# An alignment directive ahead of attention's second product, in an attention and channel-mix kernel

## The chip, the cores and the metric

The kernel runs on one core of a Trainium2 chip. The metric is the device time of one execution in microseconds, the median of several runs; lower is better. TensorE (PE in the profile) multiplies, and its weight loads are shown apart (PEld); VectorE is DVE, ScalarE is ACT, GpSimd is POOL, and SyncE (SP) issues the transfers.

## The reference

Attention over pooled keys and values feeds an RWKV channel mix. Batch 8, 8 heads, 576 tokens, head size 64; keys and values are averaged over groups of 8, which leaves 72 keys for each head.

```python
k_p = k.reshape(B, H, Sp, pool, D).mean(axis=3)
v_p = v.reshape(B, H, Sp, pool, D).mean(axis=3)
scores = scale * np.matmul(q, k_p.transpose(0, 1, 3, 2))
attn = softmax(scores)                       # over the 72 keys
x = np.matmul(attn, v_p)                     # (B, S, 512) after heads are joined
x_prev = x shifted by one token, zero at each batch's first
xk = mu_k * x + (1.0 - mu_k) * x_prev
xr = mu_r * x + (1.0 - mu_r) * x_prev
k = np.maximum(xk @ w_k, 0.0)                # 512 -> 1024
v = k * k @ w_v                              # 1024 -> 512
r = 1.0 / (1.0 + np.exp(-(xr @ w_r)))        # 512 -> 512
out = r * v
```

## The kernel before

The 4608 tokens are worked through in 13 chunks: 128, 256, and eleven of 384 tokens (chunks 2 to 12). For a chunk, attention comes first. `scores` multiplies queries by keys (line 769, tile `quad`), a softmax follows on DVE, ACT and POOL, and `quarters(c)` multiplies the weights of attention by the values: attention's second product (line 1000). It is written as one burst of 96 small matmuls, on quarters of the PE array, one after the other with nothing between; its operands are f32. I call the burst that makes chunk c "burst c"; there are eleven, 2 to 12.

Out of the burst's result ACT, POOL and DVE make the shifted mixes xk and xr, each split in a high and a low part so that products can run in the faster f32r format with three terms (`terms`). Then PE multiplies for the mix. `hidden(c, jt)` for jt 0 to 7 is x times w_k, 12 matmuls of 384 columns each (line 1146, tile `mm`); `gate(c, tt)` is x times w_r, 36 for a chunk (line 1195); `mixed(c, tt)` is the product by w_v, 72 for a chunk (line 1228).

The order of instructions is set while the kernel is written out. Each of these functions is a generator that gives its engine and an assumed length, and `Order.run` picks by due times which goes next. On PE this comes to a fixed round for chunks 4 to 11: `hidden(c, 0)` to `hidden(c, 7)`, burst c+1, `gate(c, ...)`, the first two thirds of `mixed(c, ...)`, a block of `scores`, the rest of `mixed`, and in some chunks a second block of scores. A burst starts right behind `hidden(c, 7)` and the gate starts right behind the burst. Every engine works its own instructions in order.

`hidden(c, jt)` takes one of three PSUM banks named `mm`; its matmuls for jt 4 first wait for DVE to have emptied that bank.

Of the kernel before, what the change touches and what calls it, by code (L numbers as in the profile page):

```python
# [25 lines left out]
NCT = DM // P  # L26
NJT = DF // P
# [4 lines left out]
CHUNKS = [128, 256] + [384] * 11  # L32
# [80 lines left out]
}  # L113
PLAN = ""
SPARE = 0.5
SECOND = 0.0
NEXT = 14.0
ATT = [0.0, 10.0]
# [117 lines left out]
def dve(n, lock=True):  # L236
    return "dve", 0.067 + n / 960, lock


def act(n, func=None):  # L240
    return "act", 0.1 + n / 1200, False, func
# [6 lines left out]
def pe(n, whole=False, times=1):  # L248
    return "pe", times * (2 * max(0.111, n / 1200 + 0.003) if whole else max(0.111, n / 2400 + 0.0135)), False
# [3 lines left out]
def attention_then_channel_mix(  # L253
# [13 lines left out]
    nc = tc.nc  # L267
# [41 lines left out]
    def operand(kind, c):  # L309
        if c in WHOLE:  # L310
            return whole_operands[kind]
        if (kind, c) not in operands:
            whole = {"pth": range(len(CHUNKS)), "xkh": WHOLE_HID, "xrh": WHOLE_GATE, "sh": WHOLE_MIX, "ptq": range(len(CHUNKS))}.get(kind, ())
            dtype = F32 if c in whole else F32R
            operands[kind, c] = sb.tile(shapes[kind], dtype, name=f"{kind}_{c}", tag=kind)
        return operands[kind, c]
# [7 lines left out]
    def before(kind, c):  # L324
        return every(kind, c - 1) if c > 1 else []

    def free_of_early(c, tag):
        kept = c in {"sl": WHOLE_MIX, "xrl": WHOLE_GATE}[tag]
        return [("early", t, i) for t, n in EARLY for i in range(n) if t == tag and not kept]
# [387 lines left out]
    def softmax(i):  # L717

        parts = tiles[i][2]
        if leads(i - 1):  # L720
            yield need(("scores", i, 0))
            yield from part(i, 0, 2)
            return
        group = [i, i + 1] if leads(i) else [i]
        if i:
            yield need(("scoring", i - 1))
            c = tiles[max(group[-1] - 2, 0)][0] - 1
            if c >= 0 and c not in WHOLE_ATT:
                yield need(("attended", c, 0))
        yield need(("q", i), *[("keys", b, p) for b, *_ in parts for p in range(1 if i in HALVED else 2)])  # L730
        pair = None
        if i in BESIDE:
            pair = [(yield take("mm")), (yield take("mm"))]
            sc = None
            halves = [t.rearrange("p (a n) -> p a n", a=1) for t in pair]
        else:
            sc = yield take("sc")
            halves = [sc[:, a:a + 1] for a in range(2)]
        held["halves", i] = sc, pair, halves
        if i in HALVED:  # L740
            for kind in ("mx", "e", "sm", "px", "pm"):
                held[kind, i] = yield take(kind)
        if leads(i):
            yield need(
                ("emptied", i - 1, 0), ("q", i + 1), *[("keys", b, p) for b, *_ in tiles[i + 1][2] for p in range(2)]
            )
            hi = yield take("hi")
            held["halves", i + 1] = hi, None, [hi[:, a:a + 1] for a in range(2)]
            order.make(("scoring", i + 1))
        order.make(("scoring", i))  # L750
        if i in HALVED:
            yield from part(i, 0, 1)
        else:
            yield from part(i, 0, 2)
# [226 lines left out]
    def quarters(c):  # L981

        yield need(*ready(c))
        sc = yield take("sc")
        hi = yield take("hi")
        yield "pe", 2.75, False
        main = operand("pth", c).rearrange("p g n -> p (g n)").rearrange("p (i j k) -> p i j k", j=16, k=32)
        rest = operand("ptq", c)
        out = quad[:, :, :CH].rearrange("p t (g i k) -> p t g i k", g=NPAIR, k=32)
        batch = [next(b for b, _, n, at in units[c] if at <= CH // 4 * t < at + n) % 2 for t in range(4)]  # L990
        for g in range(NPAIR):
            for j in range(3):
                for t, i in enumerate(batch):
                    rows = slice(32 * t, 32 * t + 32)
                    for m in range(2):
                        if j < 2:
                            w, p = vq_main[i][rows, (t - 2 * m - j) % 4, g], main[rows, :, 4 * g + 2 * m + j, :]
                        else:
                            w, p = vq_rest[i][rows, g // 2, 2 * (g % 2) + m], rest[rows, :, g // 2, :]
                        nc.tensor.matmul(  # L1000
                            out=out[m * D:(m + 1) * D, t, g], lhsT=w, rhs=p, start=(j == 0), stop=(j == 2),
                        )
        for g in range(NPAIR):
            held["out", c, g] = quad[:, :, g * CH // 4:(g + 1) * CH // 4]
            order.make(("attended", c, g))
        held["quad", c] = [sc, hi, NPAIR]
# [117 lines left out]
    def hidden(c, jt):  # L1124
        n = CHUNKS[c]
        whole = c in WHOLE_HID
        if jt:
            yield need(("hiding", c, jt - 1))
        elif c > 1:
            yield need(("mixing", c - 1, CHUNKS[c - 1] // P - 1))  # L1130
        yield need(("full" if whole else "parts", "k", jt), *([("x", c, 0, 0)] if c < 2 else []))
        bank = yield take("mm")
        order.make(("hiding", c, jt))
        hp = bank[:, :n]
        for ct in range(NCT):
            yield need(("x", c, ct, 0))
            o = slice(ct * P, (ct + 1) * P)
            yield pe(n, whole, 1 if whole else 3)
            if whole:
                terms = [(full["k", jt], operand("xkh", c))]  # L1140
            else:
                h, l = high["k", jt], low["k", jt]
                xh, xl = operand("xkh", c), operand("xkl", c)
                terms = [(h, xh), (l, xh), (h, xl)]
            for k, (w, x) in enumerate(terms):
                nc.tensor.matmul(  # L1146
                    out=hp, lhsT=w[:, o], rhs=x[:, ct, :n],
                    start=(ct == 0 and k == 0), stop=(ct == NCT - 1 and k == len(terms) - 1),
                )
        order.make(("hid", c, jt))  # L1150
        yield need(*before("mixed", c), *free_of_early(c, "sl"))
        sh = operand("sh", c)[:, jt]
        kept = c in WHOLE_MIX
        rk = sh if kept else (yield take("rk"))
        yield act(n)
        nc.scalar.activation(out=rk[:, :n], in_=hp, func=AF.Relu)  # L1156
        if c < 2 and jt < SQUARED_ON_ACT[c]:
            order.give("mm", bank)
            yield act(n)
            nc.scalar.activation(out=rk[:, :n], in_=rk[:, :n], func=AF.Square)  # L1160
        else:
            yield dve(n, False)
            nc.vector.scalar_tensor_tensor(  # L1163
                out=rk[:, :n], in0=hp, scalar=0.0, in1=rk[:, :n], op0=ALU.max, op1=ALU.mult
            )
            order.give("mm", bank)
        if not kept:
            yield act(n)
            nc.scalar.copy(out=sh[:, :n], in_=rk[:, :n])  # L1169
            yield dve(n)  # L1170
            nc.vector.tensor_tensor(  # L1171
                out=operand("sl", c)[:, jt, :n], in0=rk[:, :n], in1=sh[:, :n], op=ALU.subtract
            )
            order.give("rk", rk)
        order.make(("s", c, jt))
# [76 lines left out]
    for b, i in first_tile.items():  # L1252
        c = tiles[i][0]
# [15 lines left out]
    for i in range(NT):  # L1269
        spare = SPARE if tiles[i][0] > 1 else 0.0  # L1270
        order.add(tile_due[i], softmax(i), spare)
# [6 lines left out]
    for c, n in enumerate(CHUNKS):  # L1278
        if c not in WHOLE_ATT:
            order.add(att_due[c], quarters(c), SPARE)  # L1280
        for g in range(NPAIR):
            order.add(att_due[c] + g, attended(c, g), SPARE if c > 1 else 0.0)
            if c in WHOLE:
                order.add(att_due[c] + g + 6, later_joined(c, g))
        for jt in range(NJT):
            order.add(begin[c] + 0.0455 * n * jt / NJT, hidden(c, jt), 1.0 if c else 0.0)
        for tt in range(n // P):
            order.add(begin[c] + 0.0455 * n + 2.8 * tt, gate(c, tt))
            order.add(begin[c] + (0.0455 + 0.022) * n + 5.5 * tt, mixed(c, tt))
# [56 lines left out]
```

## Time and profile before

| | us |
|---|---|
| runs | 613.98, 614.94, 616.98 |
| median | 614.94 |
| span of the profiled execution, first to last instruction | 612.4 |

Of the profiled execution the span is what is given; the median run lies 2.5 us over it, which is taken as what lies around the span. PE is busy for 592.1 us of it, DVE for 354.3, ACT for 296.1 and POOL for 221.4.

In the views, `L1000 PE MATMUL quad<-pth,vq_main` is line 1000's matmul that writes tile `quad` out of `pth` and `vq_main`. `[1.52 <-issue]` says that the engine was idle for 1.52 us before this instruction and that the profile shows nothing that it waited for. An f32 matmul runs as two loads and two products, an f32r one as one of each. Queue q8 of the DMA engines carries PE's instructions to it.

### The profile page before, as it was taken

The numbers are of one execution on the slowest core, as the hardware profiler recorded it, in microseconds if no ns is written. First come the engines' busy times: TensorE is split into PE (matmuls) and PEld (weight loads), VectorE is DVE, ScalarE is ACT, GpSimd is POOL, SyncE is SP. The second block draws the span as 40 slices with busy tenths as digits, with TensorE's granted clock in tenths as the row PEclk, the third lists the DMA queues.
The fourth block names the chain that finished last, engine by engine and source line by source line (L and its number), as shares of the span: only waits on it lengthen the run. The fifth ranks groups of instructions, "written<-read, shape, count | busy, mean of one in ns | idle before, by whom it ended". The sixth has DMA issues, their size and how long they took to land.

```text
span 612.4 us, 13988 instructions
## 1 busy us (share of the span) xinstructions
PE 592.1 (97%) x5822; PEld 508.9 (83%) x5822; DVE 354.3 (58%) x709; ACT 296.1 (48%) x574; POOL 221.4 (36%) x350
## 2 busy tenths in 40 slices
PE   9989999999999899999999999999999999999997
PEld 8868457888989888988988987988977977988985
DVE  5779975976537927727726816956516825423411
ACT  3656765845462454453644444544435436335420
POOL 2411259548151555524125525355105306105000
PEclk9999999999999999999999999999999999999999
DMA  8697332342004134212005205032002000000001
GB/s 307 218 344 296 108 119 69 131 165 89 9 18 182 44 105 164 88 44 104 2 2 181 87 27 182 19 130 70 19 2 70 18 2 35 17 2 36 18 0 51
DMA packets 23054, 54.70 MB, mean 89 GB/s; under 512 B 2896, under 2 KB 6352, under 8 KB 22992
## 3 DMA queue, kind: packets, MB, share of 16 engines
q1 hardware_dynamic: 22992, 53.82, 24.9%
q8 instruction: 45, 0.74, 0.5%
q14 instruction: 17, 0.14, 0.1%
HBM read 41.23 MB, written 9.44 MB: 83 GB/s over the span
## 4 chain that ended last, share of the span: by engine, by line
PE 73%; POOL 9%; DVE 6%; issue 5%; ACT 5%; DMA 0%; POOLq 0%; DVEq 0%; ACTq 0%
PE mm L1146 31%; PE mm L1228 16%; PE mm L1195 14%; PE quad L1000 4%; POOL xkl L1120 3%; POOL xrl L1120 3%; PE quad L769 3%; DVE xm L1094 3%; ACT t L1052 2%; ACT xkh L1118 1%; PE bank L441 1%; PE mm L578 1%; POOL stage L567 1%; ACT xrh L1118 1%; PE quad L1038 1%
## 5 line engine op out<-in xcount | busy, mean ns | idle before, releaser
L1146 PE MATMUL mm<-xkh,w_k 128*128 128x384 f32 x704 | 180.1, 336 | 0.3 <-DVE rk L1163 0.2
L1228 PE MATMUL mm<-w_v,sh 128*128 128x512 f32 x528 | 167.2, 392 | 0.0
L1146 PEld LDWEIGHTS mm<-xkh,w_k 128*128 128x128 f32 x704 | 126.7, 188 | 2.3 <-DVE rk L1163 0.5
L1094 DVE SCALAR_TENSOR_TENSOR xm<-quad,given,t 128x384 f32<-128x384 f32 x88 | 50.4, 613 | 126.4 <-ACT t L1052 89.6
L1146 PE MATMUL mm<-xkl,w_k 128*128 128x384 f32 x352 | 117.9, 335 | 0.5 <-POOL xkl L1120 0.5
L1228 PEld LDWEIGHTS mm<-w_v,sh 128*128 128x128 f32 x528 | 99.1, 188 | 21.4
L1228 PE MATMUL mm<-w_v,sl 128*128 128x512 f32 x264 | 102.9, 390 | 0.0
L1195 PE MATMUL mm<-w_r,xrh 128*128 128x512 f32 x264 | 84.3, 394 | 3.0 <-issue 1.6
L1169 ACT CAST sh<-rk 128x384 fp32r<-128x384 f32 x88 | 45.1, 513 | 64.3 <-DVE rk L1163 64.1
L1156 ACT ACTIVATE rk<-mm 128x384 f32<-128x384 f32 x88 | 43.1, 490 | 66.5 <-PE mm L1146 65.3
L1171 DVE TENSOR_TENSOR sl<-rk,sh 128x384 fp32r<-128x384 f32 x88 | 56.0, 636 | 28.4 <-ACT sh L1169 27.8
L1120 POOL TENSOR_TENSOR xkl<-xm,xkh 128x384 fp32r<-128x384 f32 x44 | 44.2, 1016 | 65.2 <-ACT xkh L1118 65.2
L1146 PEld LDWEIGHTS mm<-xkl,w_k 128*128 128x128 f32 x352 | 66.1, 188 | 1.1 <-POOL xkl L1120 1.1
L1195 PEld LDWEIGHTS mm<-w_r,xrh 128*128 128x128 f32 x264 | 49.5, 188 | 12.9 <-issue 1.7
L1163 DVE SCALAR_TENSOR_TENSOR rk<-mm,rk 128x384 f32<-128x384 f32 x88 | 48.6, 553 | 19.6 <-ACT rk L1156 19.5
L567 POOL TENSOR_TENSOR stage<-stage 128x512 f32<-128x512 f32 (+4 forms) x56 | 51.0, 913 | 20.2 <-issue 9.1
L1228 PEld LDWEIGHTS mm<-w_v,sl 128*128 128x128 f32 x264 | 49.6, 188 | 10.0
L1203 ACT ACTIVATE rs<-mm 128x512 f32<-128x512 f32 x36 | 21.5, 599 | 66.4 <-PE mm L1195 66.3
L1052 ACT ACTIVATE t<-quad,om_sb 128x384 f32<-128x384 f32 (+1 forms) x96 | 48.3, 573 | 7.7 <-PE quad L1000 4.0
L1195 PE MATMUL mm<-w_r,xrl 128*128 128x512 f32 x132 | 51.4, 390 | 0.0
L1238 DVE TENSOR_TENSOR rs<-mm,rs 128x512 f32<-128x512 f32 x36 | 24.7, 687 | 41.4 <-PE mm L1228 41.1
L856 POOL TENSOR_TENSOR px<-e,sm 128x64 f32<-128x64 f32 (+1 forms) x33 | 11.6, 352 | 102.3 <-DVE sm L850 89.4
(138 smaller groups left out, 784.4 us busy)
## 6 DMA issues: line engine op xcount, KB each, us to landing
qs<-in_qT SPq DMA_DIRECT2D x36, 256.0 KB, 3.8
out<-rs SPq DMA_DIRECT2D x36, 256.0 KB, 2.0
stage<-in_kT SPq DMA_DIRECT2D x15, 576.0 KB, 4.9
stage<-in_vm SPq DMA_DIRECT2D x15, 512.0 KB, 5.5
got_wk<-in_w_k SPq DMA_DIRECT2D x8, 512.0 KB, 7.2
got_wv<-in_w_v SPq DMA_DIRECT2D x8, 512.0 KB, 10.0
stage<-in_vr SPq DMA_DIRECT2D x6, 512.0 KB, 3.9
got_wr<-in_w_r SPq DMA_DIRECT2D x4, 512.0 KB, 7.3
```

The lines of the kernel that those rows point to most:

```text
L567: nc_eng.tensor_tensor(out=st[:, :, :w], in0=st[:, :, :w], in1=st[:, :, w:2 * w], op=ALU.add)
L1052: nc.scalar.activation(out=by_token(ts[m][:, 1:n + 1]), in_=xp, func=AF.Copy, scale=om_sb[:, m, g:g + 1])
L1094: nc.vector.scalar_tensor_tensor(out=by_token(xm[:, :n]), in0=bank[:, :n] if c in WHOLE_ATT else bank, scalar=mu_sb[:, m, g:g + 1], in1=by ...
L1120: nc.gpsimd.tensor_tensor(out=lo, in0=xm[:, :n], in1=hi, op=ALU.subtract)
L1146: nc.tensor.matmul(out=hp, lhsT=w[:, o], rhs=x[:, ct, :n], start=(ct == 0 and k == 0), stop=(ct == NCT - 1 and k == len(terms) - 1),)
L1156: nc.scalar.activation(out=rk[:, :n], in_=hp, func=AF.Relu)
L1163: nc.vector.scalar_tensor_tensor(out=rk[:, :n], in0=hp, scalar=0.0, in1=rk[:, :n], op0=ALU.max, op1=ALU.mult)
L1169: nc.scalar.copy(out=sh[:, :n], in_=rk[:, :n])
L1171: nc.vector.tensor_tensor(out=operand("sl", c)[:, jt, :n], in0=rk[:, :n], in1=sh[:, :n], op=ALU.subtract)
L1195: nc.tensor.matmul(out=bank, lhsT=x[:, ct, o], rhs=w, start=(ct == 0 and k == 0), stop=(ct == NCT - 1 and k == len(terms) - 1),)
L1228: nc.tensor.matmul(out=bank, lhsT=s[:, o], rhs=w, start=(jt == 0 and k == 0), stop=(jt == NJT - 1 and k == len(terms) - 1),)
L1238: nc.vector.tensor_tensor(out=rs, in0=bank, in1=rs, op=ALU.mult)
```

## The change

One directive on TensorE, in front of the first matmul of `hidden(c, 4)` for chunks 4 to 11, thus eight times, ahead of bursts 5 to 12. As the directive is defined, the loader of the program puts padding there, so that the instruction behind it comes to stand at a given slot of a block of 256 instructions. Up to 64 slots of padding are run as empty instructions; where more are needed, the first of them is made a branch over the rest.

The slot asked for is (45 - 96) mod 256 = 205. From there `hidden(c, 4)` to `hidden(c, 7)` issue 4 x 12 matmuls, each one load and one product: 96 instructions. The burst behind them begins at slot 45.

```diff
+BLOCK = 256
+ALIGNED_FROM = 4
+INTO_BLOCK = 45
+MOST_PADS = 64
@@ hidden(c, jt)
             yield need(("x", c, ct, 0))
             o = slice(ct * P, (ct + 1) * P)
             yield pe(n, whole, 1 if whole else 3)
+            if c >= ALIGNED_FROM and 2 * jt == NJT and ct == 0 and c + 1 < len(CHUNKS):
+                before_quarters = 3 * 2 * NCT * (NJT // 2)
+                nc.tensor.addr_align(BLOCK, (INTO_BLOCK - before_quarters) % BLOCK, MOST_PADS)
             if whole:
```

PE's order is otherwise as it was. On PE, before, where `hidden(4, 3)` ends and `hidden(4, 4)` begins (chunk 4; `mm` are the banks, `xkh` and `xkl` the parts of xk, `w_k` parts of the weights; what an instruction waits for stands behind it):

```order
L1146 MATMUL mm_118<-xkh_1872,w_k_648 128x384 x2
L1146 MATMUL mm_118<-xkl_1873,w_k_648 128x384
L1146 MATMUL mm_117<-xkh_1872,w_k_657 128x384 [waits DVE_49]
L1146 MATMUL mm_117<-xkh_1872,w_k_657 128x384
L1146 MATMUL mm_117<-xkl_1873,w_k_657 128x384
```

The same place on PE now (seven lines further down in the source); the directive is the row `ISA`:

```order
L1153 MATMUL mm_118<-xkh_1872,w_k_648 128x384 x2
L1153 MATMUL mm_118<-xkl_1873,w_k_648 128x384
L1145 ISA
L1153 MATMUL mm_117<-xkh_1872,w_k_657 128x384 [waits DVE_49]
L1153 MATMUL mm_117<-xkh_1872,w_k_657 128x384
L1153 MATMUL mm_117<-xkl_1873,w_k_657 128x384
```

The directive stands ahead of the matmul that waits for DVE. Further on, now as before, the end of `hidden(4, 7)` and the start of burst 5 on PE:

```order
L1153 MATMUL mm_117<-xkl_1873,w_k_713 128x384
L1153 MATMUL mm_117<-xkh_1872,w_k_713 128x384 x2
L1153 MATMUL mm_117<-xkl_1873,w_k_713 128x384
L1004 MATMUL quad<-pth_1817,vq_main_71 64x96 x4
L1004 MATMUL quad<-pth_1817,vq_main_72 64x96 [waits DMAHW3_49]
```

No instruction stands between the two but what the rows show, so nothing moved here but by the padding.

## Rows read from the trace of the kernel before

**Rows 1.** the page: busy time by engine, instruction queue, the last chain by engine.

```profile
PE 592.1 (97%) x5822; PEld 508.9 (83%) x5822; DVE 354.3 (58%) x709; ACT 296.1 (48%) x574; POOL 221.4 (36%) x350
...
q8 instruction: 45, 0.74, 0.5%
...
PE 73%; POOL 9%; DVE 6%; issue 5%; ACT 5%; DMA 0%; POOLq 0%; DVEq 0%; ACTq 0%
```

**Rows 2.** waits of PE, 160 to 560 us: us in total, times, longest.

```profile
PE quad L769 <- DVE xm L1094: 4.0, 7, 0.7
PE quad L1000 <- issue: 2.7, 2, 1.3
PE mm L1195 <- issue: 1.6, 1, 1.6
PE mm L1195 <- DVE ptq L923: 1.4, 1, 1.4
```

**Rows 3.** the last chain in order of time: start us, us, what; bursts 5, 7, 8, 10, 11.

```profile
208.13 2.56 PE quad L1000 x151
210.69 1.55 issue
212.25 8.48 PE mm L1195 x36
...
303.12 2.54 PE quad L1000 x145
305.65 8.42 PE mm L1195 x36
...
348.98 2.12 PE quad L1000 x124
...
353.23 8.40 PE mm L1195 x36
...
443.95 2.38 PE quad L1000 x136
...
447.90 8.36 PE mm L1195 x36
...
492.51 2.39 PE quad L1000 x137
...
496.65 8.40 PE mm L1195 x36
```

**Rows 4.** timeline of the weight loads in bursts 8 and 10.

```profile
350.68 0.23 PEld L1000 LDWEIGHTS quad<-pth,vq_main 32*64 32x64 f32 x7
352.43 0.28 PEld L1000 LDWEIGHTS quad<-pth,vq_main 32*64 32x64 f32 x19 [1.52 <-issue]
...
446.42 0.19 PEld L1195 LDWEIGHTS mm<-w_r,xrh 128*128 128x128 f32 x1
447.90 0.19 PEld L1195 LDWEIGHTS mm<-w_r,xrl 128*128 128x128 f32 x1 [1.30 <-issue]
```

**Rows 5.** L1000 alone in burst 5: stretch us, PE busy (x), PEld busy (x), clock.

```profile
208.00:212.24 4.24, 2.63 (x192) 2.44 (x192) 1.00 0.01 4
```

**Rows 6.** instruction queue in 210.0:211.1 and in 395:398.07: packets, MB, share.

```profile
q8 instruction: 1, 0.02, 5.4%
...
q8 instruction: 1, 0.02, 2.6%
```

**Rows 7.** the last chain: hidden of chunk 5, then the scores behind bursts 5 and 7.

```profile
232.31 1.23 PE quad L769 x64
...
239.24 16.67 PE mm L1146 x96
...
325.41 1.23 PE quad L769 x64
```

**Rows 8.** from burst 5 to burst 6 and burst 7 to burst 8: all engines, clock.

```profile
208.06:255.84 47.78, 45.51 (x461) 40.33 (x461) 30.27 (x54) 21.03 (x41) 28.34 (x43) 1.00 0.34 117
303.05:348.91 45.86, 45.39 (x462) 40.31 (x461) 26.47 (x51) 20.65 (x38) 19.20 (x28) 1.00 0.25 90
```

## The prediction

> **What bounds the kernel now.** I read the page first. PE is busy for 592.1 of 612.4 us, and the chain that ended last lies on PE for 73% [rows 1]. A microsecond of PE's idle time in the steady part is therefore close to a microsecond of the whole. So the next view is what PE waits for, from 160 to 560 us, which holds bursts 4 to 12. Four rows carry nearly all of it [rows 2]: scores that wait for DVE, 4.0 us in 7 times, and three rows that add up to 2.7 + 1.6 + 1.4 = 5.7 us in 4 times, at the bursts (L1000) or at the first matmul behind one (L1195). Three of those four waits are put down to "issue": nothing that the profile shows was waited for.
>
> The last chain in order of time says where they are [rows 3]. An ordinary burst takes 305.65 - 303.12 = 2.53 us until the gate starts. The other bursts look like it but for four: burst 5 takes 4.12, burst 8 353.23 - 348.98 = 4.25, burst 10 3.95 and burst 11 4.14 us. Their excess is 1.59 + 1.72 + 1.42 + 1.61 = 6.34 us.
>
> In burst 8 the pause stands in the middle of a run of loads of one kind that wait for nothing [rows 4]. In burst 10 the profile names DVE ptq [rows 2], but the load of that very product ran at 446.42, and it is the load that carries the wait. The product and the next load came at 447.90 [rows 4]. So that too is a pause between two instructions, not a wait for DVE.
>
> **What the pause is.** I counted PE's instructions in program order: a load one, a product one, a separate semaphore instruction one. A burst is 192 loads and 192 products [rows 5], 384 instructions. The whole is 11,690, and queue q8 brings them in 45 packets of 0.74 MB together [rows 1], one for every 256 or so. The first instruction behind each of the four pauses is number 4290, 7106, 9154 and 10178 in this count. Their differences are 2816, 2048 and 1024, which are 11, 8 and 4 times 256. So all four pauses stand on the same slot, where a block of 256 begins. From this the starting slots of bursts 2 to 12 follow: 86, 69, 102, **128**, 25, 51, **204**, 230, **127**, **153**, 242, the four that pause in bold.
>
> A burst issues an instruction each 2.53 / 384 = 6.6 ns, a block in 1.69 us. Burst 5 starts at 208.06 us [rows 8] in slot 128, passes a boundary after 128 instructions, at 208.9, and reaches the next at its own end, 1.69 us later. One packet comes in 210.0 to 211.1 us, with 5.4% of 16 engines for 1.1 us, thus 0.95 us long [rows 6], and PE goes on at 212.25 [rows 3]. So the block behind a boundary opened 3.3 us after the boundary before it; the same sum gives 3.2, 3.2 and 3.1 for bursts 8, 10 and 11. My reading: a block is ordered when the one before it is entered, takes 3.1 to 3.3 us, and only a burst eats a block faster than that.
>
> Bursts 9 and 12 also pass two boundaries (26 and 14 instructions in) and don't pause. For burst 9 a packet lies within 395 to 398.07 us [rows 6], before its first product at 398.07: the instructions had been taken in ahead of the array, so the order went out early. This lead matters below.
>
> The page Runtime: NRT & Kernel Launch of the Trainium skill, section Instruction fetch mechanics, says that crossing a boundary is mostly hidden, since instructions are issued more slowly than blocks arrive. By that rule there would be nothing to gain and the sum would stay at 614.9. The trace agrees for nearly all of the 45 blocks and not for these four, where the measured pauses decide.
>
> **The change, term by term.**
>
> *Bursts 5 to 12 begin at slot 45.* The 96 instructions behind the directive end there, and I found nothing else between. The boundary ahead is then 45 instructions, 22.5 matmuls of `hidden`, before the burst: 16.67 / 96 = 0.174 us each [rows 7], thus 3.9 us. The one boundary within is 211 instructions in, 1.4 us. Between them lie 5.3 us, against 3.3 needed. The next is 173 instructions of burst and 41.5 of gate's products of 8.42 / 36 = 0.234 us [rows 3] later: 1.1 + 9.7 = 10.8 us. No pause is left by this: **-6.3 us**. Bursts 6 and 7, at slots 25 and 51, ran without a pause on either side of 45. An error of a few slots in my count would not matter. Bursts 6, 7, 9 and 12 move too, and gain nothing.
>
> *Padding.* By the same count the directive has to fill 173, 103, 230, 103, 230, 103, 230 and 167 slots, always more than 64, so each is a branch over the rest. Its cost is not in the trace before, since no branch stands in PE's steady part. Below, nothing: a product of `hidden` takes 0.174 us, `hidden(c, 3)` alone queues 12, 2.1 us, in front of the branch, and burst 9 shows that instructions are taken in ahead by more than 1 us. Above, each branch costs a whole late block with no cover, 8 x 3.3 = 26.4 us. I take **0**: the nearest rows are the boundaries crossed within `hidden`, which leave no pause of PE in [rows 2]. The cover is gone if PE's instructions are not ahead there, so a branch is paid from the point where it exceeds the lead. The five that skip fewer land in their own block, which is held; the three that skip 230 land in the next, which was ordered 231 instructions earlier. Behind a branch the block ends after 51 instructions, 25.5 products or 4.4 us, so an order that goes out at the branch (3.3 us) is also in time.
>
> The page named above, same section, says that a taken branch to a block that isn't held makes it be fetched before execution goes on. By this rule a branch within its own block is free, and one into a block still on its way is paid.
>
> *More blocks.* 1339 slots of padding are 5.2 blocks, so about 5 packets more on q8, 0.95 us each on one of 16 engines: nothing that PE waits for.
>
> *What comes back.* Behind a burst the chain of ACT, POOL and DVE leads to the next scores, where PE waits in 7 of 8 cases [rows 2]. If that chain started at the burst, PE, coming 1.6 us sooner, would wait there instead. It does not: from the gate's start to the scores it is 232.31 - 212.25 = 20.06 us in paused chunk 5 and 325.41 - 305.65 = 19.76 in unpaused chunk 7 [rows 3, 7]. The gate's start sets it, pause or not, so the scores move along with the gate. The 0.3 us between them recurs in chunks 5, 8 and 11 and looks like their place in the batches. It makes up the rest of 47.78 - 45.86 = 1.92 us by which the stretch from burst 5 exceeds that from burst 7 with as many products [rows 8]. If it goes as well, the gain is 7.2; I don't count it. Clock: 1.00 in both stretches [rows 8], the higher of its levels, so fewer pauses can't raise it.
>
> **Sum.** 612.4 - 6.3 = 606.1 us of span. The median of the runs lies 2.5 us over the span: **608.6 us**, 1.0% less.
>
> **The rivals.**
> 1. *The branches are paid* (slower). At 1 us each the sum is 614.9 - 6.3 + 8 = 616.6, at 3.3 each 635. It decides from 6.3 / 8 = 0.8 us each. For it: eight branches where none were, in `hidden`, where every product is on the path. Against it: the queued products of `hidden` and the lead at burst 9. 11 in 100.
> 2. *Nothing changes, 614.9 us*: the pauses aren't blocks, or the slots come out otherwise. For it: the profile calls the pause "issue" and no view names a cause. Against it: four pauses on one slot of 256, each with a packet in it. Branches that just eat the gain end here too. 8 in 100.
> 3. *Half comes back* at the scores: 614.9 - 3.2 = 611.7. For it: 4.0 us waited there already. Against it: the equal distance from the gate. 4 in 100, about half of it on either side of 0.5%.
> 4. My forecast, with its own range 607.2 to 610.2 (down to 614.9 - 7.2 = 607.7 and 0.5 for the spread of the runs; up to 0.2 us paid per branch, 608.6 + 1.6): 77 in 100.
>
> 0.5%, 3.1 us, is about what a measurement here can tell from no change. Faster by more 0.79, within it 0.10, slower 0.11. The range goes from 606.8 to 612.0, over forecast and rival 3.
>
> **What would show it.** Right: bursts 5, 8, 10 and 11 take 2.54 us from first product to gate like the others; the three L1195 and L1000 rows of [rows 2] are gone; the wait of scores for DVE stays near 4.0 us; q8 has about 50 packets; `hidden(c, 4)` starts with no gap. Wrong: a new idle time of PE in front of `hidden(c, 4)` or within the next 51 instructions, where the block behind the branch ends (rival 1), pauses that stay or wander to other instructions (rival 2), or a longer wait of L769 for DVE (rival 3).

## The result and the profile after

The changed kernel takes 608.36 us (median of 5 runs, 607.99 to 609.06), against 616.07 (613.98 to 616.98, 5 runs) before: 0.988 of it, with an interval of 0.986 to 0.990. The profiled execution has a span of 606.2 us instead of 612.4.

The page of the changed kernel, its busy times and the instruction queue:

```profile
PE 591.7 (98%) x5822; PEld 508.9 (84%) x5822; DVE 354.8 (59%) x709; ACT 296.0 (49%) x574; POOL 222.2 (37%) x350
...
q8 instruction: 51, 0.84, 0.6%
```

PE's busy time is as before but for 0.4 us [rows 1]. So nearly all of the 6.2 us is idle time that went. The queue brings 6 blocks more. What PE waits for from 160 to 560 us is now one row; of [rows 2] the three rows at the bursts are gone, and the scores' wait is as it was, 3.9 for 4.0:

```profile
PE quad L773 <- DVE xm L1098: 3.9, 7, 0.7
```

The last chain in order of time (L1004 is the burst, L1202 the gate, L773 the scores):

```profile
208.36 2.57 PE quad L1004 x152
210.93 8.40 PE mm L1202 x36
...
230.90 1.23 PE quad L773 x64
...
301.63 2.54 PE quad L1004 x151
304.17 8.40 PE mm L1202 x36
...
323.89 1.23 PE quad L773 x64
...
347.46 2.57 PE quad L1004 x152
350.03 8.40 PE mm L1202 x36
...
440.73 2.54 PE quad L1004 x154
443.27 8.40 PE mm L1202 x36
...
487.90 2.54 PE quad L1004 x152
490.44 8.40 PE mm L1202 x36
```

Bursts 5, 8, 10 and 11 now take 2.57, 2.57, 2.54 and 2.54 us to the gate, where [rows 3] had 4.12, 4.25, 3.95 and 4.14: 6.24 us less, the whole change of the span. From the gate to the scores it is 19.97 us in chunk 5 and 19.72 in chunk 7, where [rows 3, 7] had 20.06 and 19.76.

The directive's line, and the loads around the first product behind the first directive:

```profile
L1145 PEldq COMPARE_BRANCH  x8: 168/178/316, 196.8 to 521.9; - x8
```

```profile
199.53 0.19 PEld L1153 LDWEIGHTS mm<-xkl,w_k 128*128 128x128 f32 x1
199.71 0.36 PEld L1153 LDWEIGHTS mm<-xkh,w_k 128*128 128x128 f32 x2
```

All eight directives became branches. The five that land in their own block take 168 to 187 ns, the three that skip 230 slots into the next block 275 to 316. The first ran at 196.8 us and the product behind it at 199.7: PE's instructions were taken in 2.9 us ahead of the array, and the loads at 199.53 and 199.71 follow each other in the usual 0.17 to 0.18 us. Nothing on the array shows that the branch was there.

### The profile page after: what moved, and what is told of

The parts are those of the page before. It is cut to its first block, busy times and chain, and to the rows that moved or that the text cites. A ratio compares the mean times of both kernels' runs of the same rounds, so it can differ in the third digit from the quotient of the medians.

```text
span 606.2 us, 13996 instructions
## 1 busy us (share of the span) xinstructions
PE 591.7 (98%) x5822; PEld 508.9 (84%) x5822; DVE 354.8 (59%) x709; ACT 296.0 (49%) x574; POOL 222.2 (37%) x350
## 4 chain that ended last, share of the span: by engine, by line
PE 71%; POOL 9%; DVE 7%; ACT 6%; issue 5%; DMA 1%; POOLq 0%; DVEq 0%; ACTq 0%
PE mm L1153 31%; PE mm L1235 16%; PE mm L1202 13%; PE quad L1004 4%; POOL xkl L1124 3%; POOL xrl L1124 3%; PE quad L773 3%; DVE xm L1098 3%; ACT t L1056 2%; POOL stage L571 1%; ACT xkh L1122 1%; PE bank L445 1%; PE mm L582 1%; ACT xrh L1122 1%; DVE stage L571 1%
## 5 line engine op out<-in xcount | busy, mean ns | idle before, releaser
L1202 PE MATMUL mm<-w_r,xrh 128*128 128x512 f32 x264 | 84.3, 393 | 0.0
L1202 PEld LDWEIGHTS mm<-w_r,xrh 128*128 128x128 f32 x264 | 49.5, 188 | 11.3
L1202 PE MATMUL mm<-w_r,xrl 128*128 128x512 f32 x132 | 51.5, 390 | 0.0
## 6 DMA issues: line engine op xcount, KB each, us to landing
got_wv<-in_w_v SPq DMA_DIRECT2D x8, 512.0 KB, 10.1
```

The lines of the kernel that those rows point to most:

```text
L1202: nc.tensor.matmul(out=bank, lhsT=x[:, ct, o], rhs=w, start=(ct == 0 and k == 0), stop=(ct == NCT - 1 and k == len(terms) - 1),)
```

## The experiments

**Where the burst begins: slots 128, 230, 120 and 204.** These differ from the changed kernel in one constant each.

```diff
-INTO_BLOCK = 45
+INTO_BLOCK = 128   # 230, 120, 204 in the other three
```

Slot 128, two boundaries in each burst:

> Bursts 5 to 12 all begin at slot 128, so each holds two block boundaries, 128 and 384 instructions in. Theory (a block takes 3.1 to 3.3 us from the entry into the one before it; a burst eats a block in 1.69 us): each of the eight pauses 1.4 to 1.6 us where the gate begins, 11 to 13 us in all, 619.5 to 621.5, slower than before. Rival A (the directive or its branch as such removed the pauses, whatever the slot): 608.4. Rival B (only something particular to chunks 5, 8, 10 and 11 pauses): four pauses, 614.9.

625.75 us, 1.017 of before (1.012 to 1.021), above the 619.5 to 621.5 expected. All eight bursts pause at the gate, in 3 + 3 + 1 + 1 times, so rivals A and B fell. The waits of PE in this run (three rows name DVE, which is as misleading as in [rows 2]: the pause stands at the same instruction in all eight):

```profile
PE mm L1202 <- DVE ptq L927: 4.8, 3, 1.7
PE mm L1202 <- issue: 4.8, 3, 2.1
...
PE mm L1202 <- DVE kbd L613: 2.1, 1, 2.1
PE mm L1202 <- DVE sl L1178: 1.4, 1, 1.4
```

That is 13.1 us, just above the 11 to 13 expected. The span, 623.4, is 17.2 over that of the changed kernel, so 4 us are something else. The windows at bursts 7, 9 and 12 and behind them (columns as in [rows 8]), and the gates behind bursts 7, 8 and 12 in the last chain:

```profile
305.00:310.40 5.40, 3.73 (x197) 3.35 (x198) 2.85 (x7) 2.29 (x3) 0.00 (x0) 1.00 0.03 6
310.40:313.80 3.40, 3.40 (x9) 2.64 (x8) 0.00 (x0) 0.10 (x1) 0.00 (x0) 0.50 0.00 0
...
405.30:412.00 6.70, 4.63 (x42) 3.71 (x29) 3.87 (x10) 2.79 (x5) 3.32 (x4) 1.00 0.69 234
...
552.75:556.15 3.40, 3.40 (x10) 2.65 (x9) 0.00 (x0) 0.00 (x0) 0.00 (x0) 0.50 0.00 0
```

```profile
309.16 10.10 PE mm L1202 x36
...
358.10 8.48 PE mm L1202 x36
...
551.61 10.06 PE mm L1202 x36
```

In two stretches of 3.4 us the granted clock is 0.50, the lower of its levels (1.2 GHz), each 1.1 to 1.2 us after a pause has ended. The two gates there take 10.1 us where the others take 8.5: 1.6 us lost each, 3.2 together; with the pauses 16.3 of the 17.2. Of the rest, 0.5 us is there before burst 5, which starts at 208.75 us instead of 208.29. The expectation had left the clock out.

Slot 230, two boundaries as well, the first 26 instructions in:

> Bursts 5 to 12 all begin at slot 230: again two boundaries in each burst, now 26 and 282 instructions in. Theory with the lead (the branches of the changed kernel ran 2.9 us ahead of the product behind them, so the first 26 instructions of a burst are taken in well ahead of the array and the order for the block goes out early, as in burst 9 of before): no pause, 608 to 609. Rival C (two boundaries in a burst pause it, wherever they stand): eight pauses of 1.6 us, 621.

608.24 us, 0.987 (0.984 to 0.991), in the range: no pause at all, one row of PE's waits as in the changed kernel. Burst 9 starts at 394.73 us here, and the instruction queue in 393 to 394.73 us reads:

```profile
q8 instruction: 1, 0.02, 3.4%
```

The block is on its way before the burst's first product. Two boundaries in a burst are thus harmless if the first is passed early enough by the part of PE that takes instructions in. Rival C fell.

Slot 120, one boundary in the burst, the next 8 instructions behind it:

> Bursts 5 to 12 all begin at slot 120: one boundary in each burst, 136 in; the next stands 8 instructions behind its end, in the gate. Theory: 248 instructions of 6.6 ns and 4 products of 0.23 us lie between, 2.5 us, against 3.1 to 3.3: pauses of 0.6 to 0.8 us in the gate, eight times, 5 to 6.5 us, 613.5 to 615. Rival D (all or nothing: only two boundaries within a burst pause it): 608.4, or full pauses, 621.

614.33 us (0.997; 0.995 to 0.998), in the range. Rival D fell. The pauses moved from the burst into the gate, `PE mm L1202 <- issue: 4.4, 8, 0.9` in PE's waits, and stand in the middle of its loads, here in chunk 8:

```profile
353.76 0.42 PEld L1202 LDWEIGHTS mm<-w_r,xrh 128*128 128x128 f32 x2
355.38 0.19 PEld L1202 LDWEIGHTS mm<-w_r,xrl 128*128 128x128 f32 x1 [1.20 <-issue]
```

A load that should follow the one before it after 0.23 us comes 1.4 us later; over the eight such pauses exceed the usual distance by 0.6 to 1.25 us, where 0.6 to 0.8 had been expected. They add up to 7.5 us in the profiled execution, which with 616.02 us is the longest of the ten. So a pause shrinks with the time that the instructions between two boundaries take. It isn't all or nothing.

Slot 204, boundaries 52 and 308 instructions in:

> Bursts 5 to 12 all begin at slot 204, boundaries 52 and 308 instructions in. Tells where the lead ends: burst 8 of before paused its full 1.7 us here. Theory without lead at 52 instructions: eight pauses of 1.6 to 1.7 us, 621 to 622. If the lead that saves slot 230 reaches 52 instructions in other chunks, fewer or shorter pauses: down to 608.4.

626.56 us, 1.017 (1.012 to 1.022), above the 621 to 622 expected. All eight pause at one place within the burst, `PE quad L1004 <- issue: 10.9, 8, 1.6`, and two stretches at 0.50 clock follow pauses here too (454.4 to 457.8 us and 505.6 to 509.0). These two cost 1.6 us each, which the expectation had left out. The lead that saves slot 230 does not reach 52 instructions into the burst, in any chunk.

**Padding run instead of jumped over.**

```diff
-MOST_PADS = 64
+MOST_PADS = 255
```

> The slots stay at 45, but up to 255 slots of padding are run as empty instructions, so no branch: 103 to 230 of them in front of hidden's fifth tile, eight times. Theory (padding is free as long as PE's own instructions are ahead by its length; the branches showed a lead of 2.9 us): free below 2.9 us / 230 = 13 ns for an empty instruction, 608.4. The nearest row is a semaphore instruction alone on PE, 51 ns: then 230 take 11.7 us and 103 take 5.3, and what exceeds 2.9 us shows, 3 x 8.8 + 3 x 2.4 + 5.9 + 5.6 = 45 us, 653. Rival (the padding as such is harmless, a branch saves nothing): 608.4.

699.87 us, 1.136 (1.133 to 1.138), longer than even the dear estimate of 653. The wait of PE, the directive's line, and the loads at the first directive:

```profile
PE mm L1153 <- issue: 72.1, 8, 13.7
```

```profile
L1145 PEldq NOP  x1339: 13/13/13, 197.7 to 615.2; - x192
```

```profile
200.42 0.19 PEld L1153 LDWEIGHTS mm<-xkl,w_k 128*128 128x128 f32 x1
210.29 0.50 PEld L1153 LDWEIGHTS mm<-xkh,w_k 128*128 128x128 f32 x2 [9.69 <-issue]
210.79 0.33 PEld L1153 LDWEIGHTS mm<-xkl,w_k 128*128 128x128 f32 x1
```

The 1339 empty instructions are the number worked out ahead. The first 173 begin at 197.7 us, and the load behind them runs at 210.29: 12.6 us, 73 ns each, although one is listed with 13. PE had work queued for 2.9 us of it; the rest is bare. The bare time is 72.1 of the 91.5 us by which this kernel is longer than the changed one. Behind such pauses the weight loads take 0.33 us instead of 0.19: the clock is low again (mean 0.943 over the run), and most of the other 19 us goes with that. The bursts start at the same slots and none pauses.

**The directive right ahead of the burst.** The slots stay, the place of the branch changes.

```diff
 # quarters(c)
+        if c > ALIGNED_FROM:
+            nc.tensor.addr_align(BLOCK, INTO_BLOCK, MOST_PADS)
         for g in range(NPAIR):
 # hidden(c, jt): the three lines of the change are taken out
```

> The directive stands right ahead of the burst instead of 96 instructions earlier, with slot 45 there. The bursts begin at the same slots; the paddings are the same eight, but each now passes a boundary, so the branch enters a new block at slot 45 and the next boundary comes 211 instructions later, 1.4 us of burst. Theory: the order goes out at the branch; with the lead of 2.9 us there are 4.3 us, no pause, and a branch of 0.17 to 0.32 us hides too: 608 to 609. With no lead at this place: eight pauses of 1.8 us and eight branches, 624.

608.74 us, 0.987 (0.986 to 0.989), in the range. The branches ran at 205.8 us and later, ahead of the bursts; burst 5 starts at 209.02:

```profile
L996 PEldq COMPARE_BRANCH  x8: 275/275/322, 205.8 to 531.5; - x8
```

```profile
209.02 0.40 PEld L1006 LDWEIGHTS quad<-pth,vq_main 32*64 32x64 f32 x32 [0.25 <-issue]
...
210.78 0.28 PEld L1006 LDWEIGHTS quad<-pth,vq_main 32*64 32x64 f32 x19 [0.31 <-issue]
```

So a lead of 3.2 us exists at the burst too. Only burst 5 pauses a little, 0.3 us, 211 instructions in, at the boundary behind the branch's block. The traffic of the DMA engines from the first branch to 208.42 us:

```profile
q1 hardware_dynamic: 130, 0.50, 68.5%
```

The packet for burst 5 starts only at 208.44 us, 2.6 us behind its branch, where the other seven start 0.9 to 1.1 us behind theirs. In the same 2.6 us behind those branches the data queue q1 takes 0 to 7% of the engines, here 68.5%. That the data held up the block is likely, but no run changes this traffic alone, so it is not shown.

**One directive of the eight**, ahead of burst 5.

```diff
-            if c >= ALIGNED_FROM and 2 * jt == NJT and ct == 0 and c + 1 < len(CHUNKS):
+            if c == ALIGNED_FROM and 2 * jt == NJT and ct == 0:
```

> Only the first of the eight directives is left, ahead of burst 5. Behind it the bursts fall as they come: 5 at 45, then 198, 224, 121, 147, 44, 70, 159 for 6 to 12. Theory: 6, 9 and 12 pause 1.5 to 1.7 us, 8 about 0.6, 7 none or up to 1.7 (between 204, which paused, and 230, which did not), 5, 10 and 11 none: 5.4 to 7.2 us, 613.8 to 615.6. Rival A (one directive, or any change of the layout, is enough): 608.4. Bursts 5, 8, 10 and 11 pause again whatever the slot: 614.9, but then with pauses in 8, 10 and 11.

614.28 us, 0.998 (0.996 to 0.999), in the range. The last chain, bursts 6 and 12, and burst 8 with the wait behind it:

```profile
255.26 2.12 PE quad L1004 x128
257.38 1.26 issue
...
349.80 2.56 PE quad L1004 x150
...
353.25 0.97 issue
...
538.87 2.37 PE quad L1004 x134
541.25 1.32 issue
```

Bursts 6, 9 and 12 pause, 8 does so in the gate, and 5, 7, 10 and 11 don't: what their slots say (7 is at 224). Before, 5, 8, 10 and 11 paused. The pauses go with the slot and not with the chunk. Rival A fell here too.

## Why the prediction was right

**The reading of the pauses** held. The pauses stand where the slots say: 24 more in the runs with slots 128, 120 and 204, four with one directive, none at 230; the one of 0.3 us with the directive at the burst stands at a boundary too. That they come from late blocks and not from the waits that the profile names is shown by moving them, with nothing else changed, into the gate (slot 120) or to the middle of the burst (204). The packets agree: in all 32 of these pauses, counting the four of before, a packet of q8 starts 0.7 to 1.6 us behind the boundary just passed and takes 0.9 to 1.5 us, and PE's next load runs 1.2 to 1.6 us behind its end.

**The gain**, 6.3 us of span, came out as 6.2; the four bursts gave back 6.24. The span was forecast at 606.1 and is 606.2.

**What lies around the span** was the loosest term. I took 2.5 us; a run of the changed kernel of 608.0 us has a span of 606.2, thus 1.8. With 1.8 the forecast would have been 607.9, 0.5 below the 608.36 measured; that 608.6 came within 0.3 is in part luck. Before's five runs have a median of 616.07, which with 1.8 means a span of 614.3, not 612.4: the execution that was profiled was one of the quick ones. So the kernel gained 7.7 us in the medians and 6.2 in the two profiles.

**The clock** was said not to matter, since it is 1.00 in [rows 8]. That is so for the execution profiled, but not for most others. Of the 26 executions of before that were timed beside the experiments, 17 have a mean granted clock of 0.994 to 0.997 and take 615.85 to 618.68 us; the nine at 0.998 to 1.0 take 614.01 to 616.07. The 13 of the changed kernel, of slot 230 and of the directive at the burst are all at 0.998 to 1.0. One stretch of 3.4 us at 0.50 lowers the mean by 0.003 and cost 1.6 us at slot 128, so one fall is about what the medians gained beyond 6.3 us. No profile of before with such a fall was kept, so it is inferred that the falls come behind its pauses.

**The arrival of a block** was given as 3.1 to 3.3 us from four pauses, with 6.6 ns for each instruction ahead of the boundary. Read off the trace, from the first instruction behind one boundary to the first load behind the next, it is 3.1 to 3.5 us for these four, and 3.1 to 3.95 for the 24 of the runs with slots 128, 120 and 204. At slot 45 5.3 us lie between, so this was harmless for the forecast. It is why slot 128 paused up to 2.1 us instead of 1.6.

**The branches** were taken as free, with 0.8 us each as the point of decision. They are free in the changed kernel, for the reason given: 2.9 us of work is queued ahead of them. The page Runtime: NRT & Kernel Launch of the Trainium skill, section Instruction fetch mechanics, says that a branch waits when its target isn't held. Here targets in their own block and in the next both cost the array nothing, which agrees; no run here branches farther. The padding itself would not have been free: run as empty instructions it costs 73 ns each, at the place where rival 1 looked for the price of the branch.

**What comes back**: nothing. The scores' wait stayed at 3.9 us because their distance from the gate did (19.97 and 19.72). The 0.3 us between chunks 5 and 7 stayed as well, 0.25, with no pause in either; it belongs to the chunk's place, as was guessed, and the gain of 7.2 was rightly left out.

No run beats the changed kernel: slot 230 and the directive at the burst lie within 0.4 us of it, inside its spread.

## What to carry to other kernels

Where PE issues hundreds of tiny matmuls in a row, it can run out of instructions. The sign is idle time of PE (up to 2.1 us here) with "issue" or an implausible engine as its cause, at instructions that differ by multiples of 256. Look at where the boundaries fall before looking for a dependency. Let no more than one of them be passed within 4 us of array time, unless the first is taken in before the burst starts, as at slot 230. Padding should be branched over, at a place where PE's instructions are well ahead of the array, and the layout has to be set anew at each burst, since one directive moves the pauses to other bursts.

## What the runs showed of the hardware that was not expected

- An empty instruction on PE, listed with 13 ns, holds up the next for 73 ns. In the changed kernel a branch within its block takes 0.17 to 0.19 us and one over 230 slots into the next block 0.28 to 0.32.
- Pauses can cost twice. Behind four of the sixteen pauses at slots 128 and 204 the granted clock fell to 0.50 for 3.4 us, 1.6 us lost each. Length alone does not decide: of the two longest at slot 128, 2.1 us each, the one at burst 12 was followed by a fall and the one at burst 9 was not (1.00 in its row above).
- The part of PE that takes instructions in was 2.9 us ahead of the array in `hidden`. That hides a branch, and the first 26 instructions of a burst, but not its first 52.
